# Splitting the first loads of q and k over two queues, and beginning four FFN1 units early, in a fused attention and FFN kernel

## The chip, the cores and the metric

The kernel runs on one core of one Trainium2 chip. The metric is the device time of one execution in microseconds; a profile's span is some 1.8 us shorter. The kernel before has two groups of times, most at 391 to 395 us or at 396 to 401 us, which turned out to matter; runs more than 1.5% above the fastest of their kernel are marked slow and left out of ratios. A run of up to some 396.7 us still counts as fast, so a ratio can mix the two groups.

## The reference, cut to what matters

```python
# q, k, v: (8 batches, 12 heads, 448, 64) fp32
scores = q @ k.T / sqrt(64)
attn   = maximum(scores, 0)**2 / 448
x      = (attn @ v), heads joined        # (3584, 768)
h      = x @ w_in                        # 768 -> 2048
g      = maximum(h, 0) + alpha * minimum(h, 0)
out    = g @ w_out                       # 2048 -> 768
```

## The kernel before

Work goes by quads (four heads; three quads make a batch). A quad's q and k are turned by TensorE (quads 0 to 5, `turn_pe`) or by a DMA transpose of a permuted copy (quads 6 on, `turn_dma`), then come scores, relu, square, A@V, and xT for FFN1. Two stretches carry the argument. The first is the start:

```python
    first = {}
    for name, src, eng in (("q", q, nc.sync), ("k", k, nc.scalar)):
        first[name] = singles.tile([128, 2, NJ * D], F32, name=f"{name}first")
        eng.dma_start(out=first[name], in_=...)          # 128 partitions x 2 x 1792 bytes
    nc.sync.dma_start(out=alpha_sb, ...)
    make_identity(nc, ident)
    load_v(0)                                            # gpsimd queue, casts to bf16
    for _ in range(36):
        nc.tensor.matmul(warm, ident, ident, start=True, stop=True)
    # q cast by VectorE in one piece, k by ScalarE in two: j 0-1, j 2-6
    ...
    for n in range(1, NG):
        load_qk(n)
        load_v(n)
    ...
    turn_pe(0, ((0, 4, "D"), (4, NJ, "D")), ((0, 2, "D"), (2, NJ, "D")))
```

The second is where the first FFN1 units begin:

```python
    early = []
    for ff in range(2):
        ps = take_bank()[:, :S]
        f1_mm(ps, 0, ff, range(4))       # needs xT of quads 0 and 1 only
        early.append(ps)
    attnv(2)                             # makes xT of quad 2: km 4 and 5
    for ff in range(2):
        f1_mm(early[ff], 0, ff, range(4, KM))
        f1_out(early[ff], 0, ff)
```

A third stretch, that the change does not touch, comes up in the experiments. In the FFN1 units of batch 1, `prepare(n)` for n = 6, 7, 8 copies q and k of a quad into a permuted buffer (`perm`, two buffers), lets the sync queue transpose it by DMA, and loads the q, k and v of quad n + 2 on the gpsimd queue. (Quad 8 is loaded twice, once by an earlier line and again by `prepare(6)`: the trace of the kernel before has 24 loads of qraw for 23 quads, the two of quad 8 issued at 54.63 and 66.72 us. All kernels here do this, and no run left the second load out.)

## Time and profile before

| | kernel before |
|---|---|
| median of the first 3 runs | 391.49 us (391.32 to 392.87) |
| span of the profile | 389.5 us |
| TensorE busy | 378.2 us |
| all waits of TensorE | 7.1 us, the last at 43.3 us |
| first scores | 7.22 us |
| xT of quad 2 waited for | 0.63 us |

TensorE is nearly always busy, so only its waits in the first 44 us can be won or lost. The lines are in the prediction.

### The profile page before, as it was taken

To read this page: it belongs to the slowest core of one execution; us is meant where nothing else is said; L and a number is where in the kernel's file an instruction comes from. 1 tells how busy PE (TensorE), PEld (TensorE's weight loads), DVE (VectorE), ACT (ScalarE), POOL (GpSimd) and SP (SyncE) were. 2 spreads that over 40 slices of the span, in tenths; PEclk is the share of its full clock that TensorE was granted. 3 is DMA by queue.
4 is the path that set the end of the run, shared out by engine and by line. 5 is a ranking of instruction groups with operands and counts; after the bars stand their busy time and mean duration, and the time that the engine had idled before them with its cause. 6 is when DMAs were issued, how large, how long until landed. Compare 5 with 4: busy or idle time off the path is not lost.

```text
span 389.5 us, 7956 instructions
## 1 busy us (share of the span) xinstructions
PE 378.2 (97%) x3228; PEld 216.0 (55%) x3228; DVE 263.9 (68%) x418; ACT 207.5 (53%) x332; POOL 65.5 (17%) x97
## 2 busy tenths in 40 slices
PE   7779999999999999999999999999999999999996
PEld 5435454555665556645655456654666546655564
DVE  3977966865777777868756687878756786735300
ACT  4966566545546546555455554655644565524311
POOL 7557212520202040202202022102000000000000
PEclk9999999999999999999999999999999999999999
DMA  9999999996859089574939259490832311120023
GB/s 181 191 202 204 206 211 206 167 195 139 134 86 144 29 129 169 82 98 73 159 89 146 55 53 176 95 153 8 164 82 51 80 24 46 42 61 2 12 72 82
DMA packets 71909, 43.75 MB, mean 112 GB/s; under 512 B 38208, under 2 KB 71872, under 8 KB 71872
## 3 DMA queue, kind: packets, MB, share of 16 engines
q0 software_dynamic: 27312, 23.04, 40.4%
q1 hardware_dynamic: 44128, 19.65, 25.7%
q8 instruction: 25, 0.41, 0.4%
q10 hardware_dynamic: 432, 0.56, 0.4%
q14 instruction: 12, 0.10, 0.1%
HBM read 47.00 MB, written 11.01 MB: 149 GB/s over the span
## 4 chain that ended last, share of the span: by engine, by line
PE 88%; ACT 5%; DVE 3%; issue 2%; DMA 1%; ACTq 0%
PE psum L252 38%; PE psum L229 36%; PE psum L169 7%; PE psum L195 6%; ACT rl L178 4%; DVE at L185 2%; DMA qfirst<-in_q_dram 1%; DVE T L147 1%; PE psum L144 1%; ACT xT L205 1%; DVE rl L180 1%; DVE gT L238 0%; ACT osb L254 0%; DVE qraw L127 0%; ACTq L260 0%
## 5 line engine op out<-in xcount | busy, mean ns | idle before, releaser
L252 PE MATMUL psum<-w_out_sb,gT 128*128 128x384 bf16 (+2 forms) x912 | 150.7, 323 | 0.2
L229 PE MATMUL psum<-xT,w_in_sb 128*128 128x448 bf16 x768 | 148.7, 353 | 1.1 <-ACT xT L205 0.6
L252 PEld LDWEIGHTS <-gT 128*128 128x128 bf16 x912 | 87.6, 98 | 61.5 <-issue 6.7
L229 PEld LDWEIGHTS <-w_in_sb 128*128 128x128 bf16 x768 | 74.2, 98 | 71.8 <-issue 4.4
L238 DVE SCALAR_TENSOR_TENSOR gT<-neg,beta_sb,psum 128x448 bf16<-128x448 f32 x128 | 84.5, 678 | 41.3 <-ACT neg L237 40.9
L237 ACT ACTIVATE neg<-psum 128x448 f32<-128x448 f32 x128 | 69.3, 546 | 70.3 <-PE psum L229 64.7
L178 ACT ACTIVATE rl<-psum 128x896 bf16<-128x896 f32 x120 | 102.9, 928 | 1.2 <-PE psum L169 1.2
L185 DVE TENSOR_TENSOR at<-rl 128x896 bf16<-128x896 bf16 x168 | 94.1, 618 | 3.5 <-ACT rl L178 3.4
L254 ACT COPY osb<-psum 128x384 f32<-128x384 f32 (+2 forms) x57 | 27.0, 474 | 97.5 <-PE psum L252 94.0
L180 DVE TENSOR_SCALAR rl<-psum 128x896 bf16<-128x896 f32 x48 | 52.1, 1086 | 37.1 <-PE psum L169 37.1
L91 POOL DMA_DIRECT2D qraw<-in_q_dram x24 | 17.2, 718 | 190.2 <-DVE perm L155 170.1
L169 PE MATMUL psum<-T 64*64 64x448 bf16 x672 | 44.7, 355 | 3.8 <-DVE T L147 1.4
L195 PE MATMUL psum<-at,vraw 64*64 64x448 bf16 x672 | 37.9, 351 | 0.7 <-ACT rl L178 0.2
L169 PEld LDWEIGHTS <-T 64*64 64x64 bf16 x672 | 20.9, 105 | 21.6 <-issue 14.6
L195 PEld LDWEIGHTS <-vraw 64*64 64x64 bf16 x672 | 24.8, 106 | 10.9 <-issue 3.7
L206 DVE TENSOR_SCALAR xT<-psum 128x448 bf16<-128x448 f32 x22 | 13.7, 625 | 14.3 <-PE psum L195 7.2
L91 POOL DMA_DIRECT2D kraw<-in_k_dram x24 | 17.3, 721 | 6.9 <-PE psum L169 3.3
L98 POOL DMA_DIRECT2D vraw<-in_v_dram x25 | 18.0, 722 | 1.2 <-DMA w_in_sb<-in_moe_w_in_dram 0.4
L205 ACT ACTIVATE xT<-psum 128x448 bf16<-128x448 f32 x22 | 12.0, 545 | 5.4 <-PE psum L195 5.4
L155 DVE COPY perm<-qraw 128x896 bf16<-128x896 bf16 x18 | 11.0, 612 | 0.4 <-DMA T<-perm 0.4
L108 POOL DMA_DIRECT2D w_in_sb<-in_moe_w_in_dram x16 | 10.0, 628 | 7.4 <-DMA vraw<-in_v_dram 2.5
L155 DVE COPY perm<-kraw 128x896 bf16<-128x896 bf16 x18 | 11.0, 609 | 0.0
(19 smaller groups left out, 35.5 us busy)
## 6 DMA issues: line engine op xcount, KB each, us to landing
out_dram<-osb SPq DMA_DIRECT2D x110, 96.0 KB, 2.3
vraw<-in_v_dram POOLq DMA_DIRECT2D x25, 224.0 KB, 7.4
qraw<-in_q_dram POOLq DMA_DIRECT2D x24, 224.0 KB, 4.8
kraw<-in_k_dram POOLq DMA_DIRECT2D x24, 224.0 KB, 6.7
w_in_sb<-in_moe_w_in_dram POOLq DMA_DIRECT2D x16, 192.0 KB, 8.7
w_out_sb<-in_moe_w_out_dram POOLq DMA_DIRECT2D x2, 1536.0 KB, 18.6
qfirst<-in_q_dram SPq DMA_DIRECT2D x1, 448.0 KB, 4.4
kfirst<-in_k_dram ACTq DMA_DIRECT2D x1, 448.0 KB, 4.7
```

The lines of the kernel that those rows point to most:

```text
L91: nc.gpsimd.dma_start(out=t.rearrange("p m j d -> p m (j d)"), in_=flat[:, 2 * g:2 * g + 2])
L155: nc.vector.tensor_copy(p[:, i], raw.pop((n, name)).rearrange("p s j d -> p j s d"))
L169: nc.tensor.matmul(ps[64 * c:64 * c + 64, r, :S], t[64 * r:64 * r + 64, 1, j, 64 * c:64 * c + 64], t[64 * r:64 * r + 64, 0, :, 64 * c:64 * ...
L178: nc.scalar.activation(rl, ps[:, :, :S], ACTF.Relu)
L180: nc.vector.tensor_scalar(rl, ps[:, :, :S], 0.0, None, ALU.max)
L185: nc.vector.tensor_tensor(a, rl, rl, ALU.mult)
L195: nc.tensor.matmul(ps[64 * s:64 * s + 64, r, :S], vv[64 * r:64 * r + 64, s, j, :], a[64 * r:64 * r + 64, s], start=(j == 0), stop=(j == NJ ...
L229: nc.tensor.matmul(ps, w_in_sb[:, km // 2, km % 2, bass.ts(ff, 128)], xT[b][:, km // 2, km % 2, :], start=(km == 0), stop=(km == KM - 1))
L237: nc.scalar.activation(neg, ps, ACTF.Relu, scale=-1.0)
L238: nc.vector.scalar_tensor_tensor(gT[b // 2][:, ff, (b % 2) * S:(b % 2) * S + S], neg, beta_sb[:, ff:ff + 1], ps, ALU.mult, ALU.add)
L252: nc.tensor.matmul(ps, gT[sb][:, ff, bass.ts(c, 128)], w_out_sb[:, hf, ff, lo:hi], start=(ff == 0), stop=(ff == KF - 1))
L254: nc.scalar.copy(o[:, lo:hi], ps)
```

## The change

The intent: get q in sooner by giving it both hardware queues before k, let k follow in two parts so that the first scores can start on the first, load quad 1 before v of quad 0, and put FFN1 work behind the last A@V of batch 0, where TensorE waits for xT. The diff, cut to its core:

```diff
-    load: q whole on sync, k whole on scalar
+    load_first(nc.sync, "q", q, slice(0, 64), 0, NJ)
+    load_first(nc.scalar, "q", q, slice(64, 128), 0, NJ)
+    load_first(nc.sync, "k", k, slice(0, 128), 0, 3)
+    load_first(nc.scalar, "k", k, slice(0, 128), 3, NJ)
...
-    load_v(0)
-    for _ in range(36):
+    for _ in range(30):
...
-    ... ("k", nc.scalar.copy, ((0, 2), (2, NJ)))
+    ... ("k", nc.scalar.copy, ((0, 3), (3, NJ)))
...
-    for n in range(1, NG):
-        load_qk(n)
-        load_v(n)
+    load_qk(1)
+    load_v(0)
+    load_qk(2)
+    load_v(1)
+    load_v(2)
...
-    turn_pe(0, ((0, 4, "D"), (4, NJ, "D")), ((0, 2, "D"), (2, NJ, "D")))
+    turn_pe(0, ((0, 4, "D"), (4, NJ, "D")), ((0, 3, "A"), (3, NJ, "D")))
...
+    todo = [(ff, km) for ff in range(4) for km in range(4)]
...
-    two units begun; attnv(2); the two ended; f1s(0, 2, 3) ahead of turn_pe(3)
+    some_early(8)       # units 0 and 1, km 0-3
+    sq()
+    attnv(2)
+    some_early(8)       # units 2 and 3, km 0-3, while xT of quad 2 is written
+    the four ended
```

More of the change, by code (lines that the diff above doesn't have):

```diff
@@ L76, in take_pair, with hold @@
         return psum[:, lo:lo + 2]
+    def hold():
+        i = min(range(8), key=lambda i: (taken[i], i))
+        taken[i] = 10**9
+        return i
     def take_bank():
@@ L112, in load_w_out, with load_first @@
         nc.gpsimd.dma_start(out=w_out_sb[:, h], in_=w_out_v[h])
-    first = {}
-    for name, src, eng in (("q", q, nc.sync), ("k", k, nc.scalar)):
-        first[name] = singles.tile([128, 2, NJ * D], F32, name=f"{name}first")
-        eng.dma_start(out=first[name], in_=src[0].rearrange("(m two) (pp j) d -> (two pp) m (j d)", two=2, j=NJ)[:, :2])
+    first = {name: singles.tile([128, 2, NJ * D], F32, name=f"{name}first") for name in "qk"}
+    def load_first(eng, name, src, p, lo, hi):
+        flat = src[0].rearrange("(m two) (pp j) d -> (two pp) m (j d)", two=2, j=NJ)
+        eng.dma_start(out=first[name][p, :, lo * D:hi * D], in_=flat[p, :2, lo * D:hi * D])
+    load_first(nc.sync, "q", q, slice(0, 64), 0, NJ)
+    load_first(nc.scalar, "q", q, slice(64, 128), 0, NJ)
+    load_first(nc.sync, "k", k, slice(0, 128), 0, 3)
+    load_first(nc.scalar, "k", k, slice(0, 128), 3, NJ)
     nc.sync.dma_start(out=alpha_sb, in_=moe_alpha.rearrange("(kf p) -> p kf", p=128))
     make_identity(nc, ident)
-    load_v(0)
     warm = psum[:, 7, :128]
-    for _ in range(36):
+    for _ in range(30):
         nc.tensor.matmul(warm, ident, ident, start=True, stop=True)
-    for name, eng, cut in (("q", nc.vector.tensor_copy, ((0, NJ),)), ("k", nc.scalar.copy, ((0, 2), (2, NJ)))):
+    for name, eng, cut in (("q", nc.vector.tensor_copy, ((0, NJ),)), ("k", nc.scalar.copy, ((0, 3), (3, NJ)))):
         t = raw_pool.tile([128, 2, NJ, D], BF16, tag=name, name=f"{name}raw")
@@ L233, in f1_out @@
     def f1_out(ps, b, ff):
-        if b % 2 == 0 and ff == 0:
+        if b // 2 not in gT:
             gT[b // 2] = g_pool.tile([128, KF, 2 * S], BF16, tag="g", name="gT")
@@ L291, with some_early @@
     load_w_out(0)
+    early = {}
+    todo = []
+    def some_early(count):
+        for ff, km in todo[:count]:
+            if ff not in early:
+                early[ff] = hold()
+            f1_mm(psum[:, early[ff], :S], 0, ff, (km,))
+        del todo[:count]
     sc(ch(2, 0, 2, "AA"))
@@ L301 @@
     sc(ch(2, 4, 7, "AAAAADA"))
+    some_early(8)
     sq()
-    early = []
-    for ff in range(2):
-        ps = take_bank()[:, :S]
-        f1_mm(ps, 0, ff, range(4))
-        early.append(ps)
-    attnv(2)
-    for ff in range(2):
-        f1_mm(early[ff], 0, ff, range(4, KM))
-        f1_out(early[ff], 0, ff)
+    attnv(2)
+    some_early(8)
+    for ff in range(4):
+        f1_mm(psum[:, early[ff], :S], 0, ff, range(4, KM))
+        f1_out(psum[:, early[ff], :S], 0, ff)
+        take(early[ff], 1)
     def f1s(b, lo, hi):
@@ L323, in prepare @@
             load_v(n + 2)
-    f1s(0, 2, 3)
     turn_pe(3)
@@ L328 @@
     load_v(6)
-    f1s(0, 3, 5)
+    f1s(0, 4, 6)
     sc(ch(3, 0, 3))
-    f1s(0, 5, 8)
+    f1s(0, 6, 8)
     sc(ch(3, 3, 6))
```

## The prediction

> **What bounds the kernel now.** I read the page first, then the list of waits of TensorE over the whole span, then the timeline of TensorE over the first 50 us, and last the chain of work that ended last, over its first 13 us.
>
> The page says that TensorE is the bound:
>
> ```profile
> PE 378.2 (97%) x3228; PEld 216.0 (55%) x3228; DVE 263.9 (68%) x418; ACT 207.5 (53%) x332; POOL 65.5 (17%) x97
> PE   7779999999999999999999999999999999999996
> DMA  9999999996859089574939259490832311120023
> ```
>
> 378.2 of 389.5 us are busy, so 11.3 us are not. The row of slices (9.7 us each) shows where: in the first three slices and the last one. From the fourth slice on no reordering of TensorE can gain anything. The DMA row is full for the first 90 us, so the order of loads could matter there too.
>
> The second view is every wait of TensorE in the whole execution (waiter, releaser, us in total, times, longest):
>
> ```profile
> PE psum L169 <- DVE T L147: 1.4, 3, 0.9
> PE psum L123 <- POOL ident masks.py:199: 1.4, 1, 1.4
> PE psum L169 <- ACT rl L178: 1.3, 3, 0.4
> PE psum L169 <- ACT xT L203: 0.8, 2, 0.4
> PE psum L229 <- ACT xT L205: 0.6, 1, 0.6
> PE psum L144 <- DVE qraw L127: 0.5, 1, 0.5
> ```
>
> All of them together make 7.1 us, all before 43.3 us, and none is on a DMA directly. DMA enters once, through the casts of the first q and k (the row of L144 waits for VectorE, which had waited for q). L169 is the scores, waiting for ScalarE and VectorE to empty PSUM; L229 is FFN1, which waits once, 0.63 us, for xT of quad 2.
>
> The third view is the chain, start and length in us, at its beginning:
>
> ```profile
> 0.74 4.37 DMA qfirst<-in_q_dram
> 5.12 0.02 issue
> 5.14 0.64 DVE qraw L127
> 5.78 0.04 issue
> 5.82 0.43 PE psum L144 x8
> 6.25 0.02 issue
> 6.28 0.90 DVE T L147 x3
> 7.18 0.04 issue
> 7.22 0.41 PE psum L169 x4
> ```
>
> The first scores start at 7.22, behind q's load, its cast, the transposes and three copies out of PSUM. After it the chain is ScalarE's relu, VectorE's squares and copies, and so on until 26.8, with ScalarE busy for 3.00 of 3.00 us from 9 to 12 and again from 12 to 15. A chain like that moves as a whole if its first link moves.
>
> The fourth is TensorE's timeline around the wait for xT:
>
> ```profile
> 22.83 1.67 PE L229 MATMUL psum<-xT,w_in_sb 128*128 128x448 bf16 x8 [0.43 <-ACT rl L178]
> 24.43 1.77 PE L195 MATMUL psum<-at,vraw 64*64 64x448 bf16 x28
> 26.82 2.05 PE L229 MATMUL psum<-xT,w_in_sb 128*128 128x448 bf16 x10 [0.63 <-ACT xT L205]
> ```
>
> Eight FFN1 matmuls (two units, km 0 to 3) run before A@V of quad 2, then TensorE has nothing until ScalarE has written xT. From 26.82 on it is never idle again but for 0.26 us at 43.3.
>
> **What the Trainium skill says.** "DMA: Bandwidth & Descriptors", Rules for kernel authors: two transfers to disjoint halves of the partitions serialise on the same 16 engines and gain no bandwidth, from one issuer or two. The trace agrees in kind: its packet records show q starting at 1.85 and k at 2.82, and from 3.0 on some 22 packets of each per 0.2 us, interleaved, 1792 bytes in 74 ns, which over 16 engines is 387 GB/s for both. So halving q over two queues buys order (q before k), not speed.
>
> The same page, Anatomy of one DMA, fits one transfer (of the gpsimd path) as 2.0 us plus bytes over 436 GB/s. Q and k together, 917,504 bytes, make 4.1 us; k, the later, landed 4.7 us after its issue. So the fit is 0.6 short here, and I add that to it.
>
> "TensorE: Matmul & The Clock Gate", Part 1: the array runs at half clock until about 3.4 us of sustained work, in a window that doesn't start with the kernel. The trace agrees: 36 warming matmuls of 128 columns took 4.00 us, 111 ns each, and the clock record starts at full clock at 5.22. Same page, Part 2: only weight loads are pulled ahead, matmuls stay in program order. The 0.63 us above are that: ready FFN1 work stood behind work that wasn't.
>
> **The change part by part.**
>
> 1. Q in two halves of 64 rows on two queues, ahead of k. Today q gets half the bandwidth from 3.0 on, and is cast at 5.14. With q first, 458,752 bytes by the fit are 3.05 us, plus 0.6, from 0.74: about 4.4. The cast (0.63) then ends at 5.0 instead of 5.77. The warming loses six matmuls: 36 less 6, by 111 ns, end at 4.7 instead of 5.36, so they don't hold the q transposes up. That is what the six are for.
>
> 2. K in two parts, j 0 to 2 and j 3 to 6. The bytes of q and k are the same, so the last k still lands near 5.3 to 5.5 (packets of 768 and 1024 bytes could make it a little worse). The first part I put at 5.0. ScalarE casts it, casts the second, and then copies T of the first (it was VectorE's job). The casts of 256 and 640 columns took 405 and 720 ns, so 0.82 ns a column and 0.195 fixed: 0.51 for 384, 0.615 for 512. The copy of 384 columns I take as 0.49, from ScalarE's 546 ns for 448 columns out of PSUM. 5.0 + 0.51 + 0.615 + 0.49 = 6.6 for the first scores, where it was 7.22. VectorE meanwhile has T of q done by about 6.1 and T of the second k part (it arrives cast at 6.1, transposed by 6.4) at 6.9; its first relu was at 7.84, so it isn't the bound. The bound of the start moves from q to k and ScalarE. Gain 0.6, between 0.2 if the first k part lands at 5.4 and 1.0 if it lands at 4.6.
>
> 3. Quad 1's q and k ahead of v of quad 0, and quad 2's ahead of v of quad 1. Each such load takes 1.15 us of the full pipe (the gpsimd queue's waits end 1.1 to 1.2 us apart: 7.83, 8.98, 10.06, 11.20). So quad 1's rows land 1.15 earlier and v of quad 0 lands 2.3 later, by about 9; its use, A@V of quad 0, is at 12.67. The wait that it could remove doesn't exist today (the transposes of quad 1 at 9.43 and 9.82 wait for no DMA), but it would appear if part 2 moved them to 8.8 and 9.2, since k of quad 1 is in by about 9.2 only. I count it as 0: it protects the 0.6.
>
> 4. FFN1: four units begun rather than two; eight more matmuls after A@V of quad 2. At 0.2 us each (2.44 us for 12) they are 1.6 us of ready work against a hole of 0.63, so the hole goes: gain 0.6. They aren't added work; units 2 and 3 do the same 12 matmuls, earlier. Banks: the two that they take are those of the score chunk (2,5), whose relu by VectorE ended at 23.6. The four units then finish two matmuls each, 0.4 us apart, while VectorE needs about 0.6 for each gT; VectorE has them done at about 30.3 instead of 29.5 for three, and the copies of T of quad 3 end near 31.4, while the scores that need them come after two more units, near 32 on the new clock. Nothing new waits there, though closely.
>
> Sum: 391.5 - 0.6 (start) - 0 (order of v) - 0.6 (hole) = 390.3. The two gains add because the chain between them (7.2 to 26.8) is ScalarE and VectorE in turn and keeps its length, and everything after 26.8 is TensorE without a break. I put 390.2, as the second relu of the start, on VectorE, also gets a copy less before it (281 ns).
>
> **The rivals.** First: the start doesn't move, since the total of q and k bytes is unchanged and k is now the last to come. For it: k was ready for ScalarE at 5.47, only 0.33 after q, and its new first part needs another cast before its copy. Against it: today VectorE does four copies in a row and the scores wait for the third; now two engines share. Then only the hole is gained, 390.9.
>
> Second: the clock. With six warming matmuls less and a gap before the transposes, the array may go to full clock a window (3.4 us) later. Transposes would then take 1.7 instead of 0.87 and a few scores twice their time: up to 0.8 us lost at the start, 391.0 with the hole. Against it: 30 matmuls are still 3.3 us and the gap is only some 0.3.
>
> Third: VectorE's and ScalarE's finishing of four units in a row delays T of quad 3, or the second group of its scores, which now comes two units (2.4 us) after the first instead of three. ScalarE had 0.5 us of idle before each neg there, so I expect it to keep up. If not, 0.3 of the hole comes back: 390.6.
>
> Fourth, to the good: the start moves by 1.0 and the better pairing of banks (units and transposes now take whole pairs) removes the 0.26 at 43.3 too: 389.5.
>
> A new wait on weights is unlikely: the first quarter of w_in was issued by 10.7 and takes 8.7, so 19.4 against a use at 22.8, and w_out's first half, issued at 31.24, took 15.0, 46.3 against 49.2.
>
> **Range and chances.** The hole is nearly sure; the start is 0.2 to 1.0. That is 389.8 to 390.7, and the three runs of before differ by 0.2 with one at +1.4. I take 389.3 to 391.1. The most that could be had is the 7.1 us of waits less the 1.4 before any work, 5.7 us or 1.5%, so over 2% faster is out of reach, and over 2% slower needs 7.8 us of new waits.
>
> **What would show it.** Right: first scores near 6.6; the wait of L229-type matmuls on xT gone from TensorE's list; first A@V near 12.1; FFN1 without a break from about 22.2. The cast of q near 4.4. Wrong: a first score at 7.2 or later; a granted clock that starts at 8 us; new waits on DMA for quad 1's k or v of quad 0; T of quad 3 in the list with more than 0.3.

## The result, and the profile after

| | before | changed |
|---|---|---|
| median, 6 runs each | 392.12 us (391.28 to 399.48) | 395.20 us (394.65 to 395.65) |
| ratio of fast runs | | 1.0082, 95% interval 1.0062 to 1.0103 |
| first scores | 7.22 us | 10.59 us |
| span | 389.5 us | 393.2 us |

A ratio is the mean time of one kernel's fast runs over that of the other's fast runs of the same rounds, so it is not quite the ratio of the medians. The change made the kernel 0.8% slower; that is clear of the noise, though under the 2% at which a kernel is called slower.

The waits of TensorE in the changed kernel (waiter, releaser, us in total, times, longest):

```profile
PE psum L157 <- ACT kraw L138: 2.9, 1, 2.9
PE psum L134 <- POOL ident masks.py:199: 1.4, 1, 1.4
PE psum L157 <- DVE qraw L138: 1.3, 1, 1.3
PE psum L182 <- ACT rl L191: 0.9, 2, 0.4
PE psum L182 <- DVE rl L193: 0.7, 1, 0.7
```

The wait for xT (L242 in this kernel's lines) is gone. In its place the transposes of k (L157) wait 2.9 us for the cast of k, which before they did not do at all, and those of q 1.3 instead of 0.5. The chain of work that ended last says why (start, length):

```profile
0.74 0.76 SPq L124
1.50 0.06 issue
1.56 7.33 DMA kfirst<-in_k_dram
8.92 0.52 ACT kraw L138
9.44 0.04 issue
9.48 1.16 PE psum L157 x14
10.64 2.69 PE psum L182 x21
```

The first part of k (the sync queue's second load), issued at 1.56, was cast only at 8.92. And the transposes of k took 1.16 us for 14, more than before. The page's slices of TensorE and of its granted clock (9.8 us each) show the reason:

```profile
PE   4979999999999999999999999999999999999996
PEclk8799999999999999999999999999999999999999
```

The clock before read 9 in every slice. The stretch 7.8 to 14.7 us, for the kernel before and then for the changed one (busy time and instructions of each engine, then clock, DMA share, GB/s):

```profile
7.80:14.70 6.90, 5.23 (x106) 3.10 (x100) 6.86 (x12) 6.90 (x9) 3.77 (x6) 1.00 1.25 193
```

```profile
7.80:14.70 6.90, 5.22 (x66) 3.12 (x66) 3.52 (x6) 4.98 (x8) 3.07 (x5) 0.51 1.43 195
```

While TensorE waited for k its clock fell to half, so in 5.2 us of busy time it did 66 matmuls instead of 106. The later FFN1 stretch did what it was meant to (compare the line at 26.82 in the prediction, with its 0.63 us of idle):

```profile
28.37 1.77 PE L208 MATMUL psum<-at,vraw 64*64 64x448 bf16 x28
30.07 3.20 PE L242 MATMUL psum<-xT,w_in_sb 128*128 128x448 bf16 x16
```

Sixteen FFN1 matmuls follow A@V without a gap. So the books of the two profiles are: first scores 10.59 - 7.22 = 3.37 us late; A@V of quad 2 starts 28.37 - 24.43 = 3.94 late, so another 0.57 went between, where the clock was half; the first FFN2 unit starts 52.66 - 49.21 = 3.45 late, so about 0.5 was won back behind A@V; from there to the end nothing changes but a tail 0.3 us longer behind the last copy (386.83 - 383.40 = 3.43 at that copy).

What happened to the four loads? The trace records each DMA packet. First and last packet of each load, and the first packet of the gpsimd queue's stream, in us:

```
kernel before    q   sync    1.85 to 4.68    256 pieces of 1792 bytes
                 k   scalar  2.82 to 5.04    256 of 1792          gpsimd stream from 5.35
changed kernel   q2  scalar  2.26 to 3.42    128 of 1792
                 q1  sync    3.04 to 4.27    128 of 1792
                 k2  scalar  3.71 to 5.19    256 of 1024 (j 3-6)
                 k1  sync    5.28 to 8.47    256 of  768 (j 0-2)  gpsimd stream from 4.77
```

The loads start one after another. All four were issued by 2.4 us, but the fourth, the 192 KB on which the first scores depend, starts at 5.28, when the gpsimd stream is already running; its packets then share the time with that stream's (from 5.6 to 6.4 us 22 to 23 and 21 to 25 of them per 0.2 us) and it takes 3.2 us. The casts start only after the last of a load's 16 completion signals, which the trace records too: for the fourth load twelve had come by 7.29 us, but the last came at 8.90. Even q gained nothing: its last packet came 0.41 us sooner than before (4.27 against 4.68), but its last signal at 5.20 instead of 5.12, and its cast starts at 5.30 instead of 5.14.

### The profile page after: what moved, and what is told of

It reads as the page before. It is cut to its first block, busy times and chain, and to the rows that moved or that the text cites. A ratio compares the mean times of both kernels' runs of the same rounds, so it can differ in the third digit from the quotient of the medians.

```text
span 393.2 us, 7947 instructions
## 1 busy us (share of the span) xinstructions
PE 379.6 (97%) x3222; PEld 216.4 (55%) x3222; DVE 263.2 (67%) x417; ACT 207.7 (53%) x333; POOL 65.7 (17%) x97
## 4 chain that ended last, share of the span: by engine, by line
PE 86%; DVE 5%; ACT 4%; DMA 2%; issue 1%; ACTq 0%; SPq 0%
PE psum L265 37%; PE psum L242 34%; PE psum L182 7%; PE psum L208 6%; ACT rl L191 3%; DVE at L198 3%; DMA kfirst<-in_k_dram 2%; PE psum L157 1%; DVE gT L251 1%; DVE rl L193 1%; DVE T L160 1%; ACT xT L218 1%; DMA out_dram<-osb 1%; ACT osb L267 0%; ACT neg L250 0%
## 5 line engine op out<-in xcount | busy, mean ns | idle before, releaser
L242 PE MATMUL psum<-xT,w_in_sb 128*128 128x448 bf16 x768 | 148.7, 353 | 0.4 <-DMA w_in_sb<-in_moe_w_in_dram 0.4
L265 PEld LDWEIGHTS <-gT 128*128 128x128 bf16 x912 | 87.7, 98 | 61.5 <-issue 6.7
L242 PEld LDWEIGHTS <-w_in_sb 128*128 128x128 bf16 x768 | 74.1, 98 | 71.4 <-issue 3.3
L182 PE MATMUL psum<-T 64*64 64x448 bf16 x672 | 45.7, 363 | 2.7 <-ACT rl L191 0.9
```

The lines of the kernel that those rows point to most:

```text
L182: nc.tensor.matmul(ps[64 * c:64 * c + 64, r, :S], t[64 * r:64 * r + 64, 1, j, 64 * c:64 * c + 64], t[64 * r:64 * r + 64, 0, :, 64 * c:64 * ...
L242: nc.tensor.matmul(ps, w_in_sb[:, km // 2, km % 2, bass.ts(ff, 128)], xT[b][:, km // 2, km % 2, :], start=(km == 0), stop=(km == KM - 1))
L265: nc.tensor.matmul(ps, gT[sb][:, ff, bass.ts(c, 128)], w_out_sb[:, hf, ff, lo:hi], start=(ff == 0), stop=(ff == KF - 1))
```

## The experiments

My theory after this: the loss is the fourth load, late in the line and then beside the gpsimd stream; the FFN1 part gains its 0.6. Rivals: the split is slow for its small pieces; the clock, with fewer warming matmuls, is the loss; the FFN1 part costs time. Experiments of a set ran on one chip, each beside runs of the kernel before; three sets made twelve kernels.

### The FFN1 part alone

```diff
 kernel before
+    the FFN1 part of the change, and nothing else
```

> The kernel before with the FFN1 part of the change alone (four units begun, eight matmuls behind the last A@V); loads, casts and order of v as before. My theory: the 0.63 us hole behind A@V of quad 2 closes and nothing else moves: 0.6 us under before, ratio 0.998 to 0.999, no TensorE wait on xT of quad 2. Rival (the four finishes in a row delay the copies of T of quad 3, or a weight is waited for): the hole comes back elsewhere, ratio 1.000 or above.

Measured: 400.27 us median (396.62 to 401.62, 6 runs), ratio 1.0137 with an interval of 1.0071 to 1.0204 (verdict: unclear; it sets six runs of the longer group against a mixture of both). The hole did close: the wait for xT is gone from the list, and FFN1 follows A@V at 26.26 without idle. But a new wait stands at its head:

```profile
PE psum L258 <- DVE gT L244: 6.5, 1, 6.5
```

It is at 84 to 91 us, far from the change. TensorE's FFN2 waits for gT of batch 1 from VectorE; VectorE itself waited (same kernel, waits of VectorE from 60 to 110 us; then the timeline):

```profile
DVE perm L161 <- DMA vraw<-in_v_dram: 11.9, 1, 11.9
```

```profile
71.01 21.84 SPq L163 DMA_TRANSPOSE T<-perm  x3
89.09 0.62 DVE L161 COPY perm<-qraw 128x896 bf16<-128x896 bf16 x1 [11.86 <-DMA vraw<-in_v_dram]
```

VectorE may write the third permuted copy only when the first DMA transpose has read its buffer. (The view names the v load, as the transfer that came last; the packet records show the first 1792 transposed packets, those of the first transpose, ending at 85.3, and the last of its 16 completion signals coming at 88.97, just before the copy at 89.09.) In the kernel before, the same wait is

```profile
DVE perm L155 <- DMA T<-perm: 0.4, 1, 0.4
```

with its first 1792 ended at 77.1 and the last signal at 77.91. From the first FFN2 matmul to the last instruction the FFN1 part alone takes 347.9 us and the kernel before 337.2, so more is lost than the wait of 6.5: the clock record has half clock from 87.7 to 97.9 us, behind the stall. So here is a second place where this kernel's time is decided, and my rival had named the right thing (time comes back elsewhere) at the wrong place. In the same set, of 51 runs of the kernel before 30 took 391.1 to 394.7 and 21 took 396.4 to 400.5. All six of this kernel lie in the range of the longer group. That the FFN1 part brings this on is not shown: with the same part and two loads, below, 8 of 20 runs were over 396.

### The loads alone

```diff
 changed kernel
-    the FFN1 part
```

> The changed kernel with the FFN1 part undone: the split loads, 30 warming matmuls, k cut at 3 and the order of v remain. My theory (the whole loss is in the loads): first scores near 10.6 us as in the changed kernel, 0.6 us slower than the changed kernel, some 3.9 us over before, ratio about 1.010. Rival (FFN1 part costs time): at or under the changed kernel, ratio 1.008 or less.

Measured: 394.47 us median (394.19 to 395.35, 14 runs), ratio 1.0041 (1.0012 to 1.0070). The hole of 0.63 us is back as expected, but the time is below that of the changed kernel, not 0.6 above, so it is the rival's number that came. The profiles speak against the rival all the same. From the start of A@V of quad 2 to the first FFN2 matmul it is 24.77 us here and 24.78 in the kernel before, but 24.29 in the changed kernel and 24.28 in the FFN1 part alone: the FFN1 part saves 0.5 there. What differs is the landing: the fourth load's last packet came at 7.40 and k was cast at 7.85, 1.1 us sooner than in the changed kernel's profile, with first scores at 9.52. The changed kernel wasn't run again on this chip; in the three profiles with this split and this stream k was cast at 7.85, 8.51 and 8.92. The loads alone lose; the size of the loss isn't fixed to better than 1 us.

### The changed kernel with the gpsimd stream held back

```diff
+    for _ in range(2):
+        nc.gpsimd.memset(idle, 0.0)     # unused tile
     load_qk(1)
     load_v(0)
```

> The changed kernel with two fills of an unused tile on GpSimd ahead of its first load, so that its stream of loads starts some 2 us or more later. Theory of sharing: the fourth load (k, j 0 to 2, on the sync queue) starts at 5.4 as now, but has the engines for itself, lands by about 6.5 instead of 8.9, first scores near 8.0 and the time is about 391.8, ratio 1.000. Rival (position in the line or descriptors alone: the fourth load is slow of itself): it still lands near 8.9, ratio 1.008 or more, as the loads behind come later too.

The stream's first packet moved to 6.10. The fourth load started at 4.94, about as late as ever, and ended at 5.94: 1.0 us alone, where it took 3.2 beside the stream. The longest issue-to-landing time of the two loads of k, for the changed kernel and then for this one:

```profile
DMA to landing us min/median/max: 4.1/5.7/7.3
```

```profile
DMA to landing us min/median/max: 4.4/4.7/5.1
```

First scores at 8.34 (8.0 expected). So the theory holds: sharing costs 2.2 us of the first scores. The 1.1 us that remain against the kernel before are the late start of the fourth load and, in part, the clock. For in this profile the clock record begins, at full clock, only at 10.71 us; before that the 14 transposes of q took 0.96 us instead of 0.58. And it has half clock again from 24.36 to 27.78 us, though TensorE had not waited for more than 1.0 us at a time since 7.2; there the eight early FFN1 matmuls took 3.14 us instead of 1.67:

```profile
24.32 3.14 PE L245 MATMUL psum<-xT,w_in_sb 128*128 128x448 bf16 x8 [0.43 <-ACT rl L194]
```

From the first cast of k to the start of A@V of quad 2 it is 20.73 us here and 18.95 with two loads (below), so 1.8 us of this profile's loss are the clock and not the loads. The median was 394.02 us (392.14 to 402.67, 22 runs; 392.86 of the 13 fast ones, 391.8 expected), ratio 1.0008 (0.9977 to 1.0039): 9 of 22 runs were over 396, so the kernel is back among those with the second group, and its fast end is not below the kernel before.

### k in halves of whole rows

```diff
-    load_first(nc.sync, "k", k, slice(0, 128), 0, 3)
-    load_first(nc.scalar, "k", k, slice(0, 128), 3, NJ)
+    load_first(nc.sync, "k", k, slice(0, 64), 0, NJ)
+    load_first(nc.scalar, "k", k, slice(64, 128), 0, NJ)
```

> The changed kernel with k split as q is, in two halves of 64 whole rows (128 pieces of 1792 bytes each) instead of 256 pieces of 768 and 256 of 1024. Theory that the loads of the two hardware queues start one after another, each after a time that grows with its number of pieces: starts near 2.2, 3.0, 3.8 and 4.6, k landed by 5.5, first scores near 7.1, time about 391.0, ratio 0.998. Rival (a fourth load falls behind the gpsimd stream whatever its pieces): k lands at 8 or later, ratio 1.006 or more.

Measured: 396.21 us median (395.18 to 398.57, 22 runs), ratio 1.0087 (1.0062 to 1.0113). My version with a time per piece is wrong: with 128 pieces in each load the starts were 2.28, 3.11, 4.05 and 5.65, the last no sooner than with 256. The gpsimd stream came early here (3.77) and the last packets of k fell at 8.84 and 9.13. Small pieces are not what makes the fourth load late; the rival's landing and ratio came. This kernel lost a further 1.28 us because ScalarE's table load came behind the wait for k (9.60), so its first scores, at 12.56, say little beyond the landing.

### q in halves, k whole

```diff
-    load_first(nc.sync, "k", k, slice(0, 128), 0, 3)
-    load_first(nc.scalar, "k", k, slice(0, 128), 3, NJ)
+    load_first(nc.scalar, "k", k, slice(0, 128), 0, NJ)
```

> The changed kernel with k in one load (on the ACT queue, third in line) instead of two; q in halves and all else as changed. Theory (each load of the hardware queues starts 0.7 to 1.7 us after the one before it, whatever its size; the one that starts after 5 shares with the gpsimd stream): k starts at 3.7 to 4.2, beside the gpsimd stream only at its end, lands by 5.9, first scores near 7.7: 3 us sooner than in the changed kernel, which is 392.2 without the slow transposes. Rival (bytes alone set the landing): k lands at 5.2 and first scores are at 7.0 or sooner. Rival (sharing with the gpsimd stream hurts a third load as much): k lands after 7.5.

Third in line, k ran from 3.93 to 6.03 and the stream started at 5.59; first scores at 7.92. That is the first theory's 7.7, and neither rival's. The median was 394.18 us (392.09 to 402.20, 20 runs), ratio 1.0043 (1.0013 to 1.0074); only the lowest runs reach the 392.2 that I had put for quick transposes. In the profiled run, of 394.04, TensorE waits 2.1 us for a DMA transpose later on.

### Two loads, the rest of the change

```diff
-    the four load_first lines
+    load_first(nc.sync, "q", q, slice(0, 128), 0, NJ)
+    load_first(nc.scalar, "k", k, slice(0, 128), 0, NJ)
```

> The changed kernel with q in one load and k in one load, as before; the cut of k at 3, T by ScalarE, 30 warming matmuls, the order of v and the FFN1 part stay. Theory: starts at 1.85 and 2.82, k landed at 5.4, first scores at 7.0 to 7.3, so 3.3 to 3.6 us sooner than the changed kernel; the whole loss at the start is in the split. The time is then 390.8 if the transposes are quick and 396 or more if they are slow, as in the FFN1 part alone. Rival (the 30 warming matmuls, the copy on ScalarE or the order of v are what delays the start): first scores at 8 or later.

Starts at 1.84 and 2.80, and the first scores where the kernel before has them:

```profile
7.21 0.95 PE L180 MATMUL psum<-T 64*64 64x448 bf16 x16 [0.23 <-ACT T L160]
```

So the split is the whole loss of the start. The 30 warming matmuls, the cut at 3, the copy of T by ScalarE and the new order of v cost nothing here, and they gain nothing either: A@V of quad 2 starts at 24.43 in both. The median was 393.05 us (390.65 to 400.98, 20 runs): 12 runs up to 393.73 and 8 from 397.06 on, two groups as said, but of the quick ones only one came to the 390.8 that I had put for them, and the others lie from 391.56 on. Ratio of the fast runs 0.9997 (0.9971 to 1.0023). The profile fell on a slow run, with the 5.7 us wait for gT.

### q whole, k in two parts

```diff
-    the four load_first lines
+    load_first(nc.sync, "q", q, slice(0, 128), 0, NJ)
+    load_first(nc.scalar, "k", k, slice(0, 128), 0, 3)
+    load_first(nc.scalar, "k", k, slice(0, 128), 3, NJ)
-    perm_pool: bufs=2
+    perm_pool: bufs=3
```

> Three loads the other way: q whole on the sync queue, k in two column parts (j 0 to 2, then 3 to 6) both on the ACT queue; third buffer for the permuted rows; FFN1 part and all else as changed. Theory (the number of loads ahead of the last one counts, not which tensor is cut): starts near 1.85, 2.8 and 3.6 to 4.2, the last part of k landed by 5.9, first scores at 7.5 to 8.0, so later than the 7.2 of two loads although the first part of k comes sooner. Rival (small pieces of k cost, or k's parts gain as intended): over 8.5, or at 6.9 or sooner.

Starts at 1.84, 2.86 and 4.68. The first part of k was complete at 4.51, sooner than k ever was, but the third load ended at 6.97 beside the stream, and the transposes of the second part stand in program order ahead of the first scores, which came at 8.40: later than the 8.0 at most that I expected. Median 393.69 us (391.47 to 396.84, 20 runs), ratio 1.0040 (1.0016 to 1.0064); in the profiled run TensorE also waits 1.3 us for a DMA transpose. Whichever tensor is cut, three loads are later than two.

### The clock: 72 warming matmuls

```diff
-    for _ in range(30):
+    for _ in range(72):
```

> The changed kernel with 72 warming matmuls instead of 30, so that TensorE stays busy until about 7 and its wait for k (until 9.5) is short enough, perhaps, for the clock to stay up. Theory: of the loss, the wait for k is the greater part and the half clock from 7.8 to 14.7 a smaller one: with full clock the scores and transposes from 9.5 to 14.7 are shorter by up to 1.4 us of TensorE time, of which most lies beside ScalarE's relus: 0.3 to 0.6 us off, about 394.7; first scores still at 9.8 to 10.6. Rival (the clock is the main loss): 2 us or more off, 393 or less.

Median 393.47 us (392.93 to 395.29, 20 runs), ratio 1.0030 (1.0008 to 1.0053); that is 1.7 under the changed kernel's median, more than I expected and less than the rival wanted. It isn't all clock: k was cast at 8.51 in this profile, 0.4 sooner than in the changed kernel's. The clock fell again, but for half as long:

```profile
7.80:14.70 6.90, 4.83 (x70) 2.75 (x70) 4.63 (x9) 5.70 (x9) 2.52 (x4) 0.75 1.44 197
```

The traces say what the clock costs. From the first cast of k to the start of A@V of quad 2 it is 19.45 us in the changed kernel, 18.98 here, and 18.95 with two loads, where the clock is full over that stretch. So the half clock costs 0.5 us in the changed kernel's profile, as I had expected, and the late cast of k (8.92 instead of 5.47) the other 3.4. The two medians differ by more than the two profiles (395.00 and 394.10 us); that k landed differently in the other runs, or on the other chip, is likely, but not shown.

### A third permuted buffer in the kernel before

```diff
-    perm_pool = ... bufs=2
+    perm_pool = ... bufs=3
```

> The kernel before with one more buffer for the permuted rows (3 instead of 2), nothing else. Of 51 runs of the kernel before in the first set, 30 took 391.1 to 394.7 and 21 took 396.4 to 400.5. Theory: the long ones are those in which the first DMA transpose is slow beside the loads of the gpsimd queue, and VectorE, which waits to overwrite its buffer, holds up the gT of batch 1. Then with a third buffer VectorE does not wait, and the group at 396 to 400 is gone or nearly so (all runs under 395). Rival (the long runs come from the granted clock or from elsewhere): the two groups stay, about 4 in 10 over 396.

Median 391.72 us, and all 20 runs between 391.29 and 395.18, while of 72 runs of the kernel before beside them 19 were over 396. The fast runs don't differ: ratio 0.9999 (0.9976 to 1.0023). Two runs lie a hair over the 395 that I had allowed. The second group is VectorE's wait on a slow DMA transpose, as the theory said. The clock is not what causes it, though where it falls behind the stall, as in the FFN1 part alone, it adds to it.

### FFN1 alone with the third buffer

```diff
 FFN1 part alone
-    perm_pool = ... bufs=2
+    perm_pool = ... bufs=3
```

> The FFN1 part alone plus the third buffer. Theory: FFN1 alone gains 0.6 us at 26 us and lost it to a stall of VectorE of 11.9 us at 77 us behind a slow transpose; without that wait it comes to 390.8, between 390.4 and 392, in most runs. Rival (the transposes themselves stay slow and the scores of batch 2 wait for T instead): TensorE waits for T at about 86 to 90 us and the time stays at 394 or above.

Median 392.14 us (390.76 to 396.60, 20 runs). Nine runs lie at 390.76 to 391.15, eight of them below the fastest run of the kernel before in the same set (391.14), so the hole's gain is there; in the others the rival holds. The profiled run, of 394.92 us, shows it: VectorE waits no more, and TensorE waits for T itself:

```profile
PE psum L175 <- DMA T<-perm: 2.1, 1, 2.1
```

Ratio of the fast runs 1.0003 (0.9973 to 1.0033).

### Two attempts to beat both

If the transpose is slow because of the loads beside it, fewer loads should help. The first takes FFN1 with the third buffer; the second takes the two-load version of the change with the third buffer. Both then put off v:

```diff
-            prepare(6 + ff // 4)               # loads q, k and v of quad n + 2
+            prepare(6 + ff // 4, v_too=False)
+    for n in range(8, 11):
+        load_v(n)
```

> Meant to beat both: the loads of the kernel before, the FFN1 part, the third buffer, and v of quads 8 to 10 loaded after all three groups of q and k of that stretch, so that fewer loads lie beside the first DMA transpose. If the slow transpose comes from the loads beside it, TensorE's wait of up to 2.1 us for T at 86 us goes and most runs are at 390.7 to 391.2, ratio 0.996 to 0.998 with few over 392. Rival (it isn't the amount of loads): about half of the runs over 391.5, as with the third buffer alone.

> The same with everything of the change but the split of the two loads: 30 warming matmuls, k cut at 3 with its first T by ScalarE, quad 1 ahead of v of quad 0, the FFN1 part; plus the third buffer and the later v. Theory: as the first scores are at 7.2 in both, within 0.2 us of the other candidate, 390.6 to 391.2. Rival (the order of v or the clock with fewer warming matmuls matters): 0.5 us or more apart from it.

The first: 390.89 us median (390.66 to 395.97, 20 runs), 16 of them at or below 391.21, against 393.90 for 71 runs of the kernel before beside it, of which 29 were over 396. Ratio of the fast runs 0.9961 (0.9933 to 0.9988); fast to the marking includes runs up to 396.7, so against the best cluster of before (from 391.17) the gain is the hole's 0.5 us, and the rest is runs that no longer fall behind. It beats both kernels. The second: 391.48 us (390.58 to 393.00), ratio 0.9978 (0.9961 to 0.9996). Seven of its runs lie at 390.58 to 390.72, level with the first, and the other 13 from 391.44 on, so the rival has its 0.6 us between the medians. Its profile, of a run at 391.44, shows a wait of 0.6 us for T at 95 us; whether the new order of v leads to that is not shown. Nor do the two profiles show a quicker transpose: the first one's packets ended at 80.5 and 82.3 us, against 77.1 in the kernel before. Leaving out the second load of quad 8, which lies in the same stretch, is untried.

## Why the prediction was wrong

It said 390.2 us, from 389.3 to 391.1; measured were 395.20.

- **Its parts 1 and 2, the loads, failed.** Part 2 said: "The bytes of q and k are the same, so the last k still lands near 5.3 to 5.5", and put the first scores at 6.6, a gain of 0.6 us. They came at 10.59, a loss of 3.4. I had read the start of k at 2.82 in the packet records, 0.97 us behind q though both were issued at 0.74, and used only the bandwidth from there on. That gap was the fact to use: loads on the two hardware queues start one after another, at 2.26, 3.04, 3.71 and 5.28 in the changed kernel. Two loads start by 2.8, three by 3.9 to 4.7, four by 4.9 to 5.7, and the first scores followed: 7.21 with two, 7.92 and 8.40 with three, 8.34 to 12.56 with four.
- **Sharing with the gpsimd stream was not in the sum.** In the kernel before, that stream starts at 5.35, just after k ends at 5.04, so the two never met and no view showed a cost. Pushed behind 5, a load of 192 KB took 3.2 us instead of the 1.0 that it takes alone.
- **Part 1's q cast near 4.4 was also wrong**: 5.30. A fit for one DMA was applied to two loads that wait their turn. Q's packets did end sooner, at 4.27 instead of 4.68, but the last completion signal came 0.93 us after them, where it had come 0.44 after; why is not shown.
- **The second rival came true in a form I had not given it.** In the changed kernel the clock rose in time (its record begins at full clock at 4.43) and fell while TensorE waited for k; it was at half from 7.8 to 14.7 and cost 0.5 us. With 30 warming matmuls and two loads the profiled start is at full clock from 5.4 us on; but with the stream held back it came only at 10.71, so that the rival isn't refuted in its own form. Whether 36 would have helped there is not shown.
- **Part 4, the FFN1 hole, was right at its place**: the wait is gone, about 0.5 of the 0.6 us is in the books of the changed kernel, and the fastest runs with it are 0.5 below those of before. What I missed is a later stage that can fall into a slower case, and did in all six runs of the FFN1 part alone. The changed kernel avoided it in its six runs: its VectorE waits 2.1 us for that buffer, not 11.9, and TensorE none.
- **Part 3, the order of v, was right at zero**: no wait on quad 1 or on v of quad 0 appeared (the 0.4 us before the first FFN1 matmul, put down to w_in, is as long as in the kernel before, where it is put down to ScalarE), and with two loads the start is as before.
- **Range.** I took the spread of the kernel before (one run at +1.4 us of three) as noise. Further runs showed a second group at 396 and over, and a spread up to 395 within the first, which stays with a third buffer and isn't explained. But the miss of 4 us is the start, not the spread.

What stays open: why the hardware queues start loads one after another at these distances (not for the number of pieces, as the halves of whole rows show), how much the landing of the fourth load varies, why the clock came late in one profile, and why the first transpose is slow in some executions and not in others. That its slowness, through the two buffers, makes the second group is shown; that the loads beside it cause it would fit the times of the last two kernels, but is not shown.

## What to carry to other kernels

Before splitting a load to get its first part sooner, look in the trace at when each load's first packet starts, not only at bandwidth: at the start of this program two loads gave earlier first scores than three, and three earlier ones than four beside the same stream, and the piece that the chain needs must not be the last. See what stream starts next, since a late load shares with it. And when a kernel's times fall in two groups, find the wait that makes the groups before judging a change of half a per cent: here one more buffer removed the slower group.

## What the Trainium skill lacked or had wrong

- "DMA: Bandwidth & Descriptors", Rules for kernel authors, advises against splitting a transfer into partition halves, as they serialise on the same engines; the runs agree that nothing is gained. It doesn't say that each further load also starts later: first packets at 2.26, 3.04, 3.71 and 5.28 us for four loads issued between 0.74 and 2.4, and first scores 3.4 us later than with two.
- The same page, Specifications, gives a first-byte latency of about 0.6 us for the sync and scalar queues and about 1 us for gpsimd. From the start of the issue to the first packet the traces show 1.1 us (first load), 2.1 (second) and 3.7 (fourth), and for the gpsimd stream at the start of the program, beside these loads, 2.3 to 3.9 (issued at 1.43 or 1.44, first packet at 3.77, 4.77 and 5.35).
- The page has nothing on how much a DMA transpose stretches beside gpsimd loads with a cast: the first transpose's packets, issued at 71.4 and 71.0, were through at 77.1 us in the kernel before and at 85.3 in the FFN1 part alone. Whether the loads beside them are the cause is not shown.
